# Reordering the start of a fused attention and MoE kernel: weight loads, transposes and v loads move, a group-finishing rule and buffer counts change

## The chip, the core and the metric

The kernel runs on one core of a Trainium2 chip. The metric is the device time of one execution in microseconds, taken as the median of several runs; lower is better. The core has five engines with instruction queues of their own, each worked through strictly in order: TensorE (PE, matmuls), VectorE (DVE), ScalarE (ACT), GpSimd (POOL) and SyncE (SP). Transfers are issued by POOL (one queue, which can also convert float32 to bfloat16 on the way) and by SP (another queue); SP also issues the transposing transfers.

## The reference

Attention with forget gates over 8 batches, 8 heads, 576 positions and 64 dimensions, followed by a two-layer MLP over the 4608 tokens:

```python
scores = scale * np.matmul(q, k.transpose(0, 1, 3, 2))
log_f = np.log(np.clip(f, 0.0001, 1.0))
cum = np.cumsum(log_f, axis=-1)
decay = cum[:, :, :, None] - cum[:, :, None, :]
scores = np.where(causal, -1000000000.0, scores + decay)
attn = softmax(scores)
x = (attn @ v).transpose(0, 2, 1, 3).reshape(4608, 512)
h = x @ w_in                      # w_in: 512 x 2048
g = h * (1.0 / (1.0 + np.exp(-h)))
out = g @ w_out                   # w_out: 2048 x 512
```

All inputs and the output are float32.

## The kernel before, in words

The decay is split into a factor of the query, which the normalisation cancels, and a factor of the key, `w_bf`, which is multiplied into v (with a column of ones for the denominator). So v needs a conversion on POOL before it is used.

**First blocks.** The first 128 positions of each batch are done as one piece for all eight heads. For batch b: `load_qk0(b)` (POOL transfers that convert to bfloat16, pool `conv`, tag `qkb`, four buffers) and `load_v0(b)`; `turn0(b, i)` transposes the query (i = 0) or key block on TensorE with 16 small matmuls (L286), and ACT or DVE copies it out (L293); `scores0` makes the scores (L320) and their exponential on ACT (L327); the causal mask is either added by a matmul beforehand (`ban0`) or multiplied in by DVE (`mask0`, L336); `convert_v0(b)` (POOL, L341) multiplies v by the key factor; `out0` (L360) is the product with v, normalised by DVE; `back0` (L390) transposes the result into the MoE's input. The query block goes into pool `qktp`, tag `qkT`, three buffers, which the units below use as well.

**Units.** The other 448 positions are done in 32 units, n = 4 b + p, a pair of heads of a batch each. `load_qk(n)` (SP, four transfers), `load_tails(b)` (SP, two transfers, the last 64 positions of q and k for a batch), `cast_qk(n)` (POOL, L400 and L404, to bfloat16, again a `qkb` buffer of `conv`), `transposes(n)` (SP, L428, one transposing transfer into a `qkT` buffer), `scores(n, c)` for c = 0, 1, 2 (L460, exponentials at L464 and L476, masks by DVE), `load_v(b, c)` and `convert_v(b, c)` for c = 0 to 3 (SP, then POOL at L414, into `vp`), `attend(n)` (L507, L516), and `back(m)` for a pair of units (L549 or transposing transfers). `prepare(n)` is called early in each unit and issues the casts, transposes and loads of later units.

**MoE.** Tokens come in 13 groups: first blocks of batches 0 to 3 (512 columns), 4 and 5 (256), 6 and 7 (256), then the rest of each batch (384) and the tails (256). `m1_chunk(g, fc)` is one of 16 hidden chunks of a group: four matmuls (L568), a tanh on ACT (L576) and a product on DVE into `gt` (L577). `m2_part(g, tb, part)` is a quarter of the second layer for 128 tokens: four matmuls (L613); after the fourth, ACT copies the result to an `osb` buffer (L623, pool `opool`) and the store is put in a list that `store` issues on POOL (L592). Every PSUM tile of these steps but the scores shares one pool, `pbig`, of four buffers. `w_in` and `w_out` are loaded in four quarters each (`load_w_in`, `load_w_out`, L190 and L194).

**Order.** The order on every engine is that of the program text. `fill(us)` puts MoE work of about that length between the attention's steps; `step` chooses between a hidden chunk and an M2 part, by how far each layer's group has come, and starts M2 of a group only when all of its hidden chunks have been put out. `two_more(b)` does the first blocks of batches b and b + 1 with MoE work between. `slot` is a fill that also issues waiting stores. The start goes: first blocks of batches 0 to 3; loads of 4 and 5 and of `w_in`; `w_out` and batches 6 and 7 on POOL; SP waits for the second quarter of `w_out` (`after`, L200) and then loads for the first units; `fill(5.0)`, `two_more(4)`, `fill(5.0)`, M2 opened, `fill(6.0, 2)`, `two_more(6)`, a last fill, and then the loop over pairs of units.

Of the kernel before, what the change touches and what calls it, by code (L numbers as in the profile page):

```python
# [11 lines left out]
BF16 = mybir.dt.bfloat16  # L12
P = 128
# [5 lines left out]
def kernel(  # L19
# [41 lines left out]
    recp = ctx.enter_context(tc.tile_pool(name="recp", bufs=2))  # L61
    xqp = ctx.enter_context(tc.tile_pool(name="xqp", bufs=2))
    tpool = ctx.enter_context(tc.tile_pool(name="tpool", bufs=3))
    opool = ctx.enter_context(tc.tile_pool(name="opool", bufs=5))
    xpool = ctx.enter_context(tc.tile_pool(name="xpool", bufs=1))
    setup_pool = tc.tile_pool(name="setup", bufs=1)
    setup = setup_pool.__enter__()
# [131 lines left out]
    def after(ap):  # L199
        nc.sync.dma_start(out=junk[0:1, 0:16], in_=ap)  # L200
# [77 lines left out]
    def turn0(b, i):  # L278
        src = qk0[b]
        if i == 0:  # L280
            qT0[b] = qktp.tile([P, NP, P], BF16, name="qkT", tag="qkT")
        dst, evac = ((qT0[b], nc.scalar.copy), (kT0[b], nc.vector.tensor_copy))[i]
        tp = pbig.tile([P, NP, NRUN, RUN], FP32, name="tp", tag="big")
        for c in range(RUN):
            for j in range(2):
                nc.tensor.matmul(  # L286
                    tp[j * D : (j + 1) * D, :, :, c].rearrange("p a r -> p (a r)"),
                    lhsT=src[:, i, c * D : (c + 1) * D],
                    rhs=sel[:, j, :],
                    start=True,  # L290
                    stop=True,
                )
        evac(  # L293
            out=dst[:, :, :].rearrange("p a t -> p (a t)"),
            in_=tp[:, :, :, :].rearrange("p a r c -> p (a r c)"),
        )
# [298 lines left out]
    def m2_part(g, tb, part):  # L595
        gt = gts[g]
        last = g == NG - 1 and tb == GW[g] // P - 1
        if last:
            if part % 2 == 0:
                pos[g, tb] = pbig.tile([P, DM // 2], FP32, name="po", tag="big")  # L600
            m0 = part // 2 * DM // 2
            m1 = m0 + DM // 2
            fcs = range(part % 2 * NFC // 2, (part % 2 + 1) * NFC // 2)
            done = part % 2 == 1
        else:
            if part == 0:
                pos[g, tb] = pbig.tile([P, DM], FP32, name="po", tag="big")
            m0, m1 = 0, DM
            fcs = range(4 * part, 4 * part + 4)
            done = part == 3  # L610
        po = pos[g, tb]
        for fc in fcs:
            nc.tensor.matmul(  # L613
                po[:, :],
                lhsT=gt[:, fc, tb * P : (tb + 1) * P],
                rhs=w_out_bf[:, fc, m0:m1],
                start=(fc == 0),
                stop=(fc == NFC - 1),
            )
        if done:  # L620
            store(len(stores) - 4)
            osb = opool.tile([P, m1 - m0], FP32, name="osb", tag="osb")
            nc.scalar.activation(out=osb[:, :], in_=po[:, :], func=ACT.Copy, scale=0.5)  # L623
            for n, (r, b, s0) in enumerate(rows_of(g, tb)):
                t0 = b * S + s0
                q_ = nc.gpsimd if not last else (nc.scalar if n == 1 else nc.sync)
                stores.append((q_, out[t0 : t0 + r.stop - r.start, m0:m1], osb[r, :]))
# [12 lines left out]
    def step():  # L640
# [10 lines left out]
        if can1 and can2:  # L651
            f1 = M1[a][1] / NFC
            f2 = (c - sum(M2_OF[:g2])) / M2_OF[g2]
            want = 3 - at["last"] if abs(f1 - f2) < 0.15 else (1 if f1 < f2 else 2)
            if want == at["last"] and at["row"] >= 2 and abs(f1 - f2) < 0.25:
                want = 3 - want
            can1 = want == 1
        kind = 1 if can1 else 2
        at["row"] = at["row"] + 1 if kind == at["last"] else 1
# [55 lines left out]
    scores0(3, bans)  # L715
    convert_v0(3)
    load_qk0(4)
    load_v0(4)
    load_w_in(2)
    load_qk0(5)  # L720
    load_v0(5)
    load_w_in(3)
    back0(0, on_act)
    out0(2)
    back0(1, on_act)
# [7 lines left out]
        nc.gpsimd.memset(t[:, :, 1, :], 0.0)  # L733
    for t in vps:
        nc.gpsimd.memset(t[0:ST, NR, :, :], 0.0)
    convert_v0(4)
    load_w_out(0)
    load_w_out(1)
    convert_v0(5)
    load_qk0(6)  # L740
    load_v0(6)
    load_qk0(7)
    load_v0(7)
    load_w_out(2)
    load_w_out(3)
    after(w_out_bf[0:1, 2 * NFC // WQ - 1, DM - 16 : DM])
    load_qk(0)
    load_tails(0)
    load_qk(1)
    load_v(0, 0)  # L750
    load_v(0, 1)
    convert_v0(6)
    convert_v0(7)
    load_qk(2)
    load_v(0, 2)
    load_v(0, 3)
    load_qk(3)
    for n in range(2):
        cast_qk(n)
        transposes(n)  # L760
    load_tails(1)
    for c in range(NM):
        convert_v(0, c)
# [27 lines left out]
    fill(6.0, 2)  # L791
    two_more(6, False)
    ready.add(2)
    fill(1.0)

    def prepare(n):

        b, p = divmod(n, NP)  # L800
        if n + 2 < NU:
            cast_qk(n + 2)
            transposes(n + 2)
        if n + 4 < NU:
            load_qk(n + 4)
        if p == 0 and b > 0 and b + 1 < B:
            load_tails(b + 1)
        if p == 1 and b + 1 < B:
            for c in range(NM):
                load_v(b + 1, c)  # L810
        if p >= 2 and b + 1 < B:
            for c in range(2 * (p - 2), 2 * (p - 1)):
                convert_v(b + 1, c)

    LAG = 13.0
# [71 lines left out]
```

The softmax here doesn't subtract the row's maximum and nothing guards it: scores larger than these inputs give would overflow.

## Time and profile before

| What | Value |
|---|---|
| median of 6 runs | 350.11 us (349.27 to 353.23) |
| profiled execution | 349.63 us |
| its span | 347.9 us |
| TensorE busy | 333.5 us (96%) |
| ACT busy | 216.7 us (62%) |
| DVE busy | 182.3 us (52%) |
| POOL busy | 128.8 us (37%) |
| bytes read from HBM | 36.85 MB |

The profiled execution is one run of the program under the hardware's profiler; times in its views count from the start of its span. The first slices of the span have the transfer engines at nine tenths, the TensorE clock is at its full value in all of them, and from about 260 us on there are few transfers left. A row of a timeline gives start, duration, engine, line, operation, output and inputs, shapes and count, and in brackets the idle time of the engine ahead of it with what ended it. A row of the waits gives the engine and line that waited, what it waited for, and total microseconds, times and the longest.

### The profile page before, as it was taken

How to read it: one execution, taken by the hardware profiler on the slowest of the kernel's cores; microseconds unless marked ns; L12 is line 12 of the kernel's file. 1: busy time of each engine (PE TensorE's matmuls, PEld its weight loads, DVE VectorE, ACT ScalarE, POOL GpSimd, SP SyncE). 2: the span in 40 equal slices, each digit the busy share in tenths (PEclk: the TensorE clock that was granted, in tenths of full speed). 3: DMA queues.
4: the chain of work that ended last, by engine and by line, in shares of the span. 5: the costliest groups of instructions: out<-in, count | busy, mean ns of one | idle time of the engine just before them, and what ended most of it. 6: DMA issues, size and time to landing. Idle time of an engine off the chain costs nothing.

```text
span 347.9 us, 8844 instructions
## 1 busy us (share of the span) xinstructions
PE 333.5 (96%) x3520; PEld 199.4 (57%) x3567; DVE 182.3 (52%) x389; ACT 216.7 (62%) x401; POOL 128.8 (37%) x227
## 2 busy tenths in 40 slices
PE   8989978999899999999999999999999999999995
PEld 3745545567656566565655666756656565555664
DVE  4764727366556556546646554645645463444340
ACT  5865624966675757759658585785865934545441
POOL 8997337274180272254235028314520000010011
PEclk9999999999999999999999999999999999999999
DMA  8999999997897397897799979579952100010012
GB/s 156 194 211 209 218 210 185 227 211 179 198 170 159 93 206 160 164 208 160 156 223 154 184 147 210 135 154 192 180 101 58 48 32 30 32 58 35 30 62 60
DMA packets 141497, 50.44 MB, mean 145 GB/s; under 512 B 132368, under 2 KB 138768, under 8 KB 141456
## 3 DMA queue, kind: packets, MB, share of 16 engines
q1 hardware_dynamic: 131440, 32.70, 51.8%
q0 software_dynamic: 9856, 17.04, 20.3%
q8 instruction: 28, 0.46, 0.6%
q10 hardware_dynamic: 160, 0.13, 0.1%
q14 instruction: 13, 0.11, 0.1%
HBM read 36.85 MB, written 9.44 MB: 133 GB/s over the span
## 4 chain that ended last, share of the span: by engine, by line
PE 81%; DMA 6%; POOL 4%; ACT 3%; issue 3%; DVE 1%; ACTq 0%; POOLq 0%
PE po L613 34%; PE hp L568 29%; PE sc L460 7%; DMA w_out_bf<-in_moe_w_out_dram 6%; PE dn L507 5%; PE dn L516 3%; PE wm L232 1%; POOL v L341 1%; ACT u L464 1%; PE tp L286 1%; POOL w_in_bf L190 1%; DVE u L336 1%; ACT ut L476 1%; POOL vf L140 1%; PE tx L549 1%
## 5 line engine op out<-in xcount | busy, mean ns | idle before, releaser
L576 ACT ACTIVATE th<-hp 128x384 bf16<-128x384 f32 (+2 forms) x208 | 95.8, 482 | 88.1 <-PE hp L568 86.0
L577 DVE SCALAR_TENSOR_TENSOR gt<-th,hp 128x384 bf16<-128x384 bf16 (+2 forms) x208 | 105.6, 522 | 78.9 <-ACT th L576 75.6
L613 PE MATMUL po<-w_out_bf,gt 128*128 128x512 bf16 (+1 forms) x550 | 138.5, 373 | 5.9 <-DMA w_out_bf<-in_moe_w_out_dram 1.9
L568 PE MATMUL hp<-x,w_in_bf 128*128 128x384 bf16 (+2 forms) x700 | 129.0, 321 | 0.5
L568 PEld LDWEIGHTS <-w_in_bf 128*128 128x128 bf16 x832 | 78.1, 98 | 53.8 <-issue 1.6
L592 POOL DMA_DIRECT2D out_dram<-osb x38 | 20.9, 551 | 176.0 <-ACT osb L623 125.8
L613 PEld LDWEIGHTS <-gt 128*128 128x128 bf16 x592 | 55.1, 98 | 52.2 <-issue 5.3
L464 ACT ACTIVATE u<-sc 128x1024 bf16<-128x1024 f32 (+1 forms) x96 | 75.3, 824 | 11.9 <-PE sc L460 11.8
L414 POOL TENSOR_TENSOR vp<-vf,w_bf 128x520 bf16<-128x520 f32 (+1 forms) x32 | 35.0, 1097 | 16.5 <-DMA vf<-in_v_dram 11.4
L469 DVE TENSOR_TENSOR u<-u,tri 128x768 bf16<-128x768 bf16 x32 | 22.2, 695 | 25.6 <-ACT u L464 25.6
L623 ACT ACTIVATE osb<-po 128x512 f32<-128x512 f32 (+1 forms) x37 | 22.2, 599 | 14.4 <-PE po L613 14.3
L460 PE MATMUL sc<-qkT 64*128 64x128 bf16 (+1 forms) x640 | 26.5, 207 | 0.1
L460 PEld LDWEIGHTS <-qkT 64*128 64x128 bf16 x640 | 18.2, 94 | 11.8 <-issue 9.1
L483 DVE TENSOR_TENSOR ut<-ut,trit 128x128 bf16<-128x128 bf16 x32 | 7.5, 233 | 31.0 <-ACT ut L476 31.0
L476 ACT ACTIVATE ut<-sc 128x640 bf16<-128x640 f32 x32 | 23.3, 729 | 0.0
L507 PEld LDWEIGHTS <-u 128*128 128x128 bf16 x576 | 20.8, 97 | 3.6 <-issue 0.3
L507 PE MATMUL dn<-vp,u 128*128 128x65 bf16 x384 | 21.8, 193 | 0.0
L525 DVE TENSOR_TENSOR xr<-dn,rec 128x448 bf16<-128x448 f32 x32 | 20.0, 625 | 1.1
L400 POOL CAST qkb<-qf 128x384 bf16<-128x384 f32 x32 | 16.2, 507 | 11.1 <-DMA qf<-in_q_dram 10.1
L507 PE MATMUL dn<-v,u 128*128 128x65 bf16 x192 | 19.8, 193 | 0.2 <-DVE gt L577 0.2
L400 POOL CAST qkb<-kf 128x384 bf16<-128x384 f32 x32 | 18.3, 571 | 1.8 <-DMA kf<-in_k_dram 1.7
L568 PE MATMUL hp<-xt,w_in_bf 128*128 128x256 bf16 x128 | 17.7, 273 | 0.1
(68 smaller groups left out, 205.6 us busy)
## 6 DMA issues: line engine op xcount, KB each, us to landing
out_dram<-osb POOLq DMA_DIRECT2D x32, 256.0 KB, 2.8
vf<-in_v_dram SPq DMA_DIRECT2D x26, 256.0 KB, 4.3
qf<-in_q_dram SPq DMA_DIRECT2D x64, 96.0 KB, 3.0
kf<-in_k_dram SPq DMA_DIRECT2D x64, 96.0 KB, 2.9
w_in_bf<-in_moe_w_in_dram POOLq DMA_DIRECT2D x4, 512.0 KB, 6.7
w_out_bf<-in_moe_w_out_dram POOLq DMA_DIRECT2D x4, 512.0 KB, 9.4
vf<-in_v_dram POOLq DMA_DIRECT2D x6, 256.0 KB, 7.0
qkb<-in_q_dram POOLq DMA_DIRECT2D x8, 128.0 KB, 5.5
```

The lines of the kernel that those rows point to most:

```text
L400: nc.gpsimd.tensor_copy(out=t2[:, c0 : c0 + NR, :].rearrange("p c x -> p (c x)"), in_=t[:, :, :, :].rearrange("p c h d -> p (c h d)"),)
L414: nc.gpsimd.tensor_tensor(out=vbf[b][r, c, :, :], in0=vst[b][c][r, :, :], in1=w_bf[r, c + 1, b * H : (b + 1) * H, None].to_broadcast([n, H ...
L460: nc.tensor.matmul(sc[:, i, o : o + q1 - q0], lhsT=kt, rhs=t[r, q0:q1], start=True, stop=True)
L464: nc.scalar.activation(out=u[:, :, c * SM : c * SM + w], in_=sc[:, :, 0:w], func=ACT.Exp, scale=scale)
L469: nc.vector.tensor_tensor(out=x, in0=x, in1=tri[:, None, None, :].to_broadcast([P, 2, NR, P]), op=ALU.mult,)
L476: nc.scalar.activation(out=ut[:, :, 0:3:2, :].rearrange("p k i t -> p i k t"), in_=sc[:, :, T0 : T0 + (NM + 1) * ST].rearrange("p i (k t) ...
L507: nc.tensor.matmul(dn[:, i * NR + c - 1, :], lhsT=u[:, i, o : o + P], rhs=vals(kb, i), start=(kb == 0), stop=(kb == c),)
L568: nc.tensor.matmul(hp[:, :], lhsT=w_in_bf[:, cc, fc * P : (fc + 1) * P], rhs=xcols(g, cc), start=(cc == 0), stop=(cc == NCC - 1),)
L576: nc.scalar.activation(out=th[:, :], in_=hp[:, :], func=ACT.Tanh, scale=0.5)
L577: nc.vector.scalar_tensor_tensor(out=gt[:, fc, :], in0=th[:, :], scalar=1.0, in1=hp[:, :], op0=ALU.add, op1=ALU.mult,)
L613: nc.tensor.matmul(po[:, :], lhsT=gt[:, fc, tb * P : (tb + 1) * P], rhs=w_out_bf[:, fc, m0:m1], start=(fc == 0), stop=(fc == NFC - 1),)
L623: nc.scalar.activation(out=osb[:, :], in_=po[:, :], func=ACT.Copy, scale=0.5)
```

## The change

Eight edits, none of which alters what is computed:

- the query blocks of the first blocks get a tag of their own, `qT0`, with two buffers in the same pool;
- the output pool has four buffers instead of five, and at most three stores are held back where it was four;
- `step` gets a rule: when at most two M2 parts are left in the groups up to the current one and the next group's hidden chunks are three quarters done, it goes on with the hidden chunks;
- the blocks of batches 4 and 5: both q and k loads first, then two quarters of `w_in`, then both v;
- all of `w_out` is issued ahead of the blocks of batches 6 and 7, its first half ahead of the conversion of batch 4's v;
- on SP and POOL, the casts and transposes of units 0, 1 and 2 stand between the loads; the v of batch 0 is loaded after the second transpose; `cast_qk(0)` stands ahead of the conversions of batches 6 and 7;
- the last fill before the units is 4.0 instead of 1.0;
- `prepare`: unit 0 no longer casts for unit 2, and the v of batch 1 is loaded at p = 2 and converted at p = 3.

```diff
-    opool = ctx.enter_context(tc.tile_pool(name="opool", bufs=5))
+    opool = ctx.enter_context(tc.tile_pool(name="opool", bufs=4))
...
-            qT0[b] = qktp.tile([P, NP, P], BF16, name="qkT", tag="qkT")
+            qT0[b] = qktp.tile([P, NP, P], BF16, name="qT0", tag="qT0", bufs=2)
...
-            store(len(stores) - 4)
+            store(len(stores) - 3)
...
                 want = 3 - want
+            if sum(M2_OF[: g2 + 1]) - c <= 2 and f1 >= 0.75:
+                want = 1
             can1 = want == 1
...
     load_qk0(4)
+    load_qk0(5)
+    load_w_in(2)
+    load_w_in(3)
     load_v0(4)
-    load_w_in(2)
-    load_qk0(5)
     load_v0(5)
-    load_w_in(3)
     back0(0, on_act)
...
-    convert_v0(4)
     load_w_out(0)
     load_w_out(1)
+    convert_v0(4)
     convert_v0(5)
-    load_qk0(6)
-    load_v0(6)
-    load_qk0(7)
-    load_v0(7)
     load_w_out(2)
     load_w_out(3)
+    load_qk0(6)
+    load_qk0(7)
+    load_v0(6)
+    load_v0(7)
     after(w_out_bf[0:1, 2 * NFC // WQ - 1, DM - 16 : DM])
     load_qk(0)
     load_tails(0)
     load_qk(1)
-    load_v(0, 0)
-    load_v(0, 1)
+    cast_qk(0)
+    transposes(0)
     convert_v0(6)
     convert_v0(7)
     load_qk(2)
-    load_v(0, 2)
-    load_v(0, 3)
+    cast_qk(1)
+    transposes(1)
+    for c in range(NM):
+        load_v(0, c)
+    cast_qk(2)
+    transposes(2)
     load_qk(3)
-    for n in range(2):
-        cast_qk(n)
-        transposes(n)
     load_tails(1)
...
     ready.add(2)
-    fill(1.0)
+    fill(4.0)
...
-        if n + 2 < NU:
+        if 0 < n < NU - 2:
             cast_qk(n + 2)
             transposes(n + 2)
         if n + 4 < NU:
             load_qk(n + 4)
-        if p == 0 and b > 0 and b + 1 < B:
+        if b + 1 == B:
+            return
+        if p == 0 and b > 0:
             load_tails(b + 1)
-        if p == 1 and b + 1 < B:
+        if p == (1 if b > 0 else 2):
             for c in range(NM):
                 load_v(b + 1, c)
-        if p >= 2 and b + 1 < B:
-            for c in range(2 * (p - 2), 2 * (p - 1)):
+        if p >= 2:
+            for c in range(2 * (p - 2), 2 * (p - 1)) if b > 0 else range(NM * (p - 2)):
                 convert_v(b + 1, c)
```

## The prediction, made before the changed kernel ran

> **What bounds the kernel now.** I read the busy table first, then TensorE's own waits, then the timelines of the engines round each wait.
>
> ```profile
> PE 333.5 (96%) x3520; PEld 199.4 (57%) x3567; DVE 182.3 (52%) x389; ACT 216.7 (62%) x401; POOL 128.8 (37%) x227
> ```
>
> TensorE is busy for 333.5 of 347.9 us. Both programs issue the same matmuls, so a change of order can win only the time in which TensorE stands still, and lose only by new waits there. The list of TensorE's waits says what there is to win:
>
> ```profile
> PE po L613 <- DMA w_out_bf<-in_moe_w_out_dram: 1.9, 1, 1.9
> PE po L613 <- issue: 1.4, 9, 0.2
> PE wm L232 <- DVE warm L204: 1.2, 1, 1.2
> PE po L613 <- DVE gt L577: 0.9, 1, 0.9
> PE dn L360 <- DVE u L336: 0.9, 2, 0.8
> PE tp L286 <- DMA qkb<-in_q_dram: 0.8, 1, 0.8
> PE tx L549 <- DVE gt L577: 0.2, 1, 0.2
> ```
>
> The columns are total us, times, longest. The "issue" row is nine gaps of one matmul's length (records that the trace lacks), and the warm-up row is before anything that changes. The other five, 4.7 us in all, are the stake. TensorE's timeline places them:
>
> ```profile
> 26.06 1.36 PE L286 MATMUL tp<-sel,qkb 128*64 128x64 bf16 x32 [0.76 <-DMA qkb<-in_q_dram]
> ...
> 41.14 2.75 PE L613 MATMUL po<-w_out_bf,gt 128*128 128x512 bf16 x12
> 43.73 0.60 PE L568 MATMUL hp<-x,w_in_bf 128*128 128x256 bf16 x4
> 46.22 1.89 PE L613 MATMUL po<-w_out_bf,gt 128*128 128x512 bf16 x7 [1.89 <-DMA w_out_bf<-in_moe_w_out_dram]
> ...
> 57.18 0.43 PE L360 MATMUL dn<-v,u 128*128 128x65 bf16 x8 [0.76 <-DVE u L336]
> ...
> 92.60 1.02 PE L613 MATMUL po<-w_out_bf,gt 128*128 128x512 bf16 x4 [0.95 <-DVE gt L577]
> ```
>
> The idle time stands in brackets ahead of the instruction that it delayed: once for a query block of batch 5, once for the last quarter of w_out, once for a mask, once at a group boundary of the MoE. After 120 us TensorE hardly waits at all.
>
> **The change, part by part.**
>
> *Loads of batch 5 ahead of w_in.* Now POOL issues qk(4), v(4), w_in(2), qk(5), v(5), w_in(3); from issue and time to landing these land at 21.9, 22.8, 25.3, 26.8, 27.5 and 29.8. So the queue lands in the order of issue, at some 2.4 us for a weight quarter (1 MB in HBM). With qk(5) straight after qk(4) its half megabyte lands near 23.3, before TensorE comes for it at 25.3. That takes away 0.76, and 0.31 more: the key block landed after the query block, and the pitch between the two transposes at 26.46 is 335 ns where 27 would do. Together -1.07. The w_in quarters then land near 25.9 and 28.3; the first use of w_in(2) is the ninth hidden chunk, at about 31. v(4) and v(5) land last, by 29.8; their conversions on POOL (1.05 each) end near 30 and 31, and out0(4) and out0(5) want them at 31.5 and 32.6. Cover of 1.5 us; beyond that each us late costs one.
>
> *w_out ahead of the first blocks of batches 6 and 7.* Landings now:
>
> ```profile
> 33.24 0.77 POOL L194 DMA_DIRECT2D w_out_bf<-in_moe_w_out_dram  x1 [0.62 <-DMA w_out_bf<-in_moe_w_out_dram]
> 35.55 0.74 POOL L194 DMA_DIRECT2D w_out_bf<-in_moe_w_out_dram  x1 [1.54 <-DMA w_out_bf<-in_moe_w_out_dram]
> ```
>
> These two landed 9.5 and 10.6 us later, at 42.7 and 46.15, behind the 1.5 MB of batches 6 and 7, which landed between 36.0 and 39.8. Changed, they are issued near 31.0 and 31.8, after the conversion of v(5), and their place in the queue is straight behind w_out(1), which lands at 35.3 as before (the same bytes are ahead of it). The trace moved the next 3.5 MB of that queue in 46.15 - 35.3 = 10.85 us, 3.1 us per MB, with SP's loads beside it. Two quarters then land at 38.4 and 41.5. TensorE needs them at 42.86 - 1.07 = 41.8 and 44.33 - 1.07 = 43.3. Here I weigh a rule: the Trainium skill's "DMA: Bandwidth & Descriptors", section "Queues, rings and completion order", says that each DMA engine takes turns, packet by packet, among the queues that have work. SP's queue opens after 35.3 in both kernels (its first load waits for w_out(1)); with a full half going to it from 36 on, a quarter would take 4.8 us, w_out(3) would land near 44.2, and 0.9 of the 1.89 would stay. The trace's 2.9 and 3.45 us between its last landings, under that very traffic, say less than a half; I take the row: -1.89.
>
> The moved blocks pay for it: qk(6) and qk(7) land near 43 and 45, v(6) and v(7) by about 46.2, since the total is unchanged. Their turns come at 49.33 - 2.96 = 46.4 and 48.8 (2.96 is what has been won so far). Nothing.
>
> *A tag of its own for qT0.* The first-block queries shared three buffers with the units' transposes, two of which are claimed in program order before batches 6 and 7. ACT shows the price:
>
> ```profile
> 53.81 0.58 ACT L293 CAST qkT<-tp 128x512 bf16<-128x512 f32 x1 [2.43 <-PE sc L320]
> 54.29 0.39 ACT L576 ACTIVATE th<-hp 128x256 bf16<-128x256 f32 x1
> 54.56 1.03 ACT L327 ACTIVATE u<-sc 128x1024 bf16<-128x1024 f32 x1
> ```
>
> The copy for batch 7 waited for the scores of batch 6, and the exponential of batch 6 queued behind it. With two own buffers the copy is done before 53, so the exponential starts when its scores end (53.7), some 0.8 earlier; the mask (1.48 each) then ends about 56.3, and TensorE comes at 56.42. -0.8 of the 0.93; batch 7's mask stays just critical.
>
> *Casts, transposes and v of the units, reordered.* SP and POOL are in order, so this needs following. SP's four loads, two tails and four loads land between 44.1 and 48.9 as now; the first cast ended at 48.6, waiting for the tails. It now stands ahead of the conversions of v(6) and v(7) (which now run at 38.2 and 39.8): 48.6 + 2 x 1.05 = 50.7. out0(6) and out0(7) come near 53.4 and 54.7. Hidden by some 4 us. Transpose 0 goes out at 48.6 instead of 55.5, four loads (2.1), transpose 1 at about 52, the four v loads to 55.6, landing by 60 with the 3.5 to 5 us of the v loads now; cast 2 ends near 57, transpose 2 goes out there, four conversions (4.6) end by 62.5 or so. The first attend of batch 0 comes at 69.8 - 3.8 + 3.0 = 69, where 3.8 is the sum of the gains so far and 3.0 the work of the next part. Hidden by 6 us. Behind them on SP stand load_qk(3), the tails of batch 1, load_qk(4) and transpose 3, going out near 65 as now (65.4), because it waits for the first unit's scores anyway. v of batch 1 is loaded one unit later and converted by about 84.5; its first attend comes near 90.
>
> *More MoE ahead of unit 0.* Three hidden chunks of 256 (0.43 each) and two M2 parts (0.86) move, 3.0 us: moved, not added. Zero.
>
> *The rule for finishing a group.* At 92.6 a new M2 tile waited 0.95 for DVE, because four hidden chunks had been put behind two score blocks and held all the four shared PSUM buffers. In the changed order the last three chunks of that group are followed by two M2 parts of the old one (1.73), which cover the tanh and the product (0.38 + 0.42). -0.95. The same for the 0.23 before the transposes at 116.67: an M2 part now stands between. The rule also makes runs of five chunks in the tail, where three were. With one buffer held by an M2 tile, three are left; for 256 columns the loop of tanh and product is about 1.0 us against 0.87 of two chunks. Bounds: nothing (a run of 20 matmuls at 153.4 takes 3.28 us with no gap) to 0.15 for each later chunk, some 0.6 in all.
>
> *Four output buffers instead of five.* ACT's copies of outputs wait for matmuls alone, never for a store; a store lands in 2.8 us and 36 token tiles take 300 us. Nothing, even where POOL holds one up.
>
> **Sum.** -1.07 - 1.89 - 0.8 - 0.95 - 0.23 = -4.94. Against it I set new waits of 0 to 1.5, 0.7 taken: the tail's runs, and unit 0, where 1.73 us of MoE instead of 2.15 stands between the first two score blocks, so that ACT's exponentials (0.93 each, two of them) are just critical. Net -4.2. The profiled execution took 349.63 (347.9 of span and 1.7 around it), so 345.4; its median was 350.11, 0.48 above, so **345.9**.
>
> **Rivals.**
>
> *The weights still come late.* With the half share the last quarter costs 0.9; with v(4) or v(5) 1 us over their cover, another 1.0. Gain 2.3: 347.8. For it: queue shares can't be read exactly from landings. Against: 2.9 and 3.45 us.
>
> *The new order brings its own waits.* ACT's exponentials around unit 0, or a run of chunks on the PSUM buffers, give back 3 to 4 us in several places: about 349.5, no change. For it: ACT is 62% busy and in order. Against: in the present kernel none of its 96 exponentials makes TensorE wait.
>
> *Slower: the chain through SP and POOL.* The conversions of batch 0's v now stand behind three casts, and their loads behind two transposes. If SP's loads are starved, each us beyond the cover of 6 at attend 0 is a us of TensorE. It ends slower by 0.5% from 6 + 4.2 + 1.8 = 12 us of lateness; at 13 us, 353. For it: SP issues of 2.2 us at 38 to 43 show a full queue. Against: at 46.2 the other queue is empty and the loads then land in 3 to 5 us.
>
> **How the numbers follow.** Forecast 0.60 (345.0 to 346.8, by the 0 to 1.5 of new waits), late weights 0.20, own waits 0.12, slower 0.08. About 0.5%, 1.8 us, is what a measurement of this kernel can tell from no change; 347.8 is faster by that bound. So faster 0.80, same 0.12, slower 0.08. The range takes in the first two cases: 344.7 to 348.6.
>
> **What will show it.** TensorE's row of waits for w_out is gone, and for qkb at turn 5; no wait of out0(6) above 0.2; no 0.9 for the product at a group's end; the third and fourth w_out quarters land by 41.8 and 43.3; transpose 0 goes out near 48.6. Wrong would be: TensorE waiting for vp or v in out0 or attend, rows for exponentials among its waits, or a start of unit 0 later than 62 us.

## The result, and the profile after

| | before | changed |
|---|---|---|
| median | 350.18 us (348.56 to 353.23, 63 runs) | 347.29 us (345.21 to 350.54, 28 runs) |
| profiled execution | 349.63 us | 347.08 us |
| its span | 347.9 us | 345.3 us |
| TensorE busy | 333.5 us | 331.4 us |

The ratio is 0.991, with a 95% interval of 0.9896 to 0.9924: 2.9 us faster by the medians. The forecast was 345.9, with a range of 344.7 to 348.6. Direction and range hold; 1.4 us of the forecast gain are missing. Three executions that ran in a slower state (one of the changed kernel, two of the weights' order alone below) are in the medians and not in the ratios, so the two can differ a little.

TensorE's busy time fell by 2.1 us although the matmuls are the same, because it counts each matmul to its modelled end; 0.8 of the 2.1 lies in the first 8 us (6.80 us busy there before, 6.00 now), ahead of every edit.

The list of TensorE's waits in the changed kernel, with total us, times and the longest:

```profile
PE sc L460 <- DMA qkT<-qkb: 2.4, 2, 1.5
PE po L613 <- issue: 1.4, 9, 0.2
PE wm L232 <- DVE warm L204: 1.2, 1, 1.2
PE dn L507 <- DVE gt L577: 1.1, 1, 1.1
PE tp L286 <- DMA qkb<-in_k_dram: 0.5, 1, 0.5
PE tp L286 <- DMA qkb<-in_q_dram: 0.3, 1, 0.3
PE tx L390 <- DVE xq L375: 0.3, 1, 0.3
PE hp L568 <- DVE gt L577: 0.2, 1, 0.2
```

The rows for `w_out` and for the mask are gone. The two `qkb` rows are not the old one: they lie at 5.5 and 6.9 us, in the first blocks of batch 0, before anything that the change touches. Three rows are new: units wait for transposed queries and keys (2.4 us), an attend waits for a product of the MoE (1.1 us), and so does a hidden chunk (0.24 us). TensorE's timeline shows the places of the old waits without a bracket, and then the new ones:

```profile
25.03 1.08 PE L286 MATMUL tp<-sel,qkb 128*64 128x64 bf16 x32
...
42.22 0.60 PE L568 MATMUL hp<-x,w_in_bf 128*128 128x256 bf16 x4
42.66 1.89 PE L613 MATMUL po<-w_out_bf,gt 128*128 128x512 bf16 x7
...
52.70 0.42 PE L360 MATMUL dn<-v,u 128*128 128x65 bf16 x8
...
60.31 0.40 PE L460 MATMUL sc<-qkT 64*128 64x128 bf16 x8
...
74.64 0.40 PE L460 MATMUL sc<-qkT 64*128 64x128 bf16 x8 [1.48 <-DMA qkT<-qkb]
...
86.23 0.40 PE L460 MATMUL sc<-qkT 64*128 64x128 bf16 x8 [0.89 <-DMA qkT<-qkb]
...
108.31 0.19 PE L507 MATMUL dn<-v,u 128*128 128x65 bf16 x1 [1.12 <-DVE gt L577]
```

The first, third and fourth rows stood at 26.06, 46.22 and 57.18 before. The fifth is the start of unit 0 (62.15 before); the sixth and seventh are the starts of units 3 and 5.

**Where the time went.** The starts of the same instruction in both timelines give the lead of the changed kernel. After the turn of batch 5 it is 28.23 - 26.92 = 1.31 us (0.20 of it was there before the turn of batch 4 already). After the last quarter of `w_out` it is 47.94 - 44.39 = 3.55, and at the second masked product 58.64 - 53.82 = 4.82. At unit 0 the changed kernel has done 3.04 us more MoE work, so the lead is 62.15 + 3.04 - 60.31 = 4.88 us, where the forecast's steps up to there made 3.8. At the end of the last matmul it is 344.04 - 341.50 = 2.54. So the start went better than forecast, and 2.3 us of the lead were lost in the units. The new brackets make 1.48 + 0.89 + 1.12 + 0.24 = 3.73 us; the old ones that are gone after unit 0 (0.95, 0.23, 0.22) make 1.40; the difference is that 2.3.

A bracket is a little less than what a wait costs. From the start of the hidden chunk at 43.73 to the M2 part at 46.22 (rows of the prediction) there were 2.49 us before; from 42.22 to 42.66 there are 0.44 now. That is 2.05 won for a bracket of 1.89: the bracket starts at the modelled end of the matmul ahead, and the next one could have started 0.16 us sooner.

**Why unit 3 waits.** Transpose 3 is the fourth of the units' transposes (they are counted from 0). These are SP's rows of the changed kernel (start, us taken to issue):

```profile
50.71 1.34 SPq L428 DMA_TRANSPOSE qkT<-qkb  x1
...
54.78 1.22 SPq L428 DMA_TRANSPOSE qkT<-qkb  x1
56.10 4.09 SPq L179 DMA_DIRECT2D vf<-in_v_dram  x4
60.28 1.54 SPq L428 DMA_TRANSPOSE qkT<-qkb  x1
...
68.41 1.67 SPq L428 DMA_TRANSPOSE qkT<-qkb  x1
...
77.47 4.68 SPq L179 DMA_DIRECT2D vf<-in_v_dram  x4
82.26 1.30 SPq L428 DMA_TRANSPOSE qkT<-qkb  x1
```

Transpose 3 goes out at 68.41 (65.42 before) and lands 6.2 us later (3.6 before): at 74.59 where it was 69.07, while TensorE comes for it at 74.64 - 1.48 = 73.16. The last thing that SP waits for ahead of it is the cast for unit 3 on POOL, as SP's waits between 66 and 70 us say:

```profile
SPq L428 <- POOL qkb L404: 0.5, 1, 0.5
```

And this is POOL's timeline up to that cast:

```profile
60.53 2.25 POOL L414 TENSOR_TENSOR vp<-vf,w_bf 128x520 bf16<-128x520 f32 x2 [3.48 <-DMA vf<-in_v_dram]
63.34 2.18 POOL L414 TENSOR_TENSOR vp<-vf,w_bf 128x520 bf16<-128x520 f32 x2 [0.55 <-DMA vf<-in_v_dram]
65.46 1.69 POOL L592 DMA_DIRECT2D out_dram<-osb  x3
67.20 0.50 POOL L400 CAST qkb<-qf 128x384 bf16<-128x384 f32 x1
```

That cast starts at 67.20 (63.68 before), straight behind the four conversions of batch 0's v, which end at 65.5 instead of 58.0, and three stores, 1.69 us. The conversions waited for their loads (3.48 and 0.55 in brackets), and those loads stand on SP behind transposes 0 and 1. So v having been moved back makes the cast late. But SP waits only 0.5 us for it: until 67.87 it is busy with the issue of the loads for units 3 and 4 and of two tails. The other 2.5 us of the later issue, and the longer flight, are not the cast's.

**Why unit 5 waits.** Transpose 5, the last row of SP above, goes out at 82.26 (77.67 before), straight behind the four loads of batch 1's v, whose issue alone took 4.68 us. They are in that place because they are loaded one unit later. It lands at 86.19; TensorE comes for it at 86.23 - 0.89 = 85.34. Whether the place of v is what makes the two transposes late is what the first experiments ask.

### The profile page after: what moved, and what is told of

It reads as the page before. It is cut to its first block, busy times and chain, and to the rows that moved or that the text cites. A ratio compares the mean times of both kernels' runs of the same rounds, so it can differ in the third digit from the quotient of the medians.

```text
span 345.3 us, 8845 instructions
## 1 busy us (share of the span) xinstructions
PE 331.4 (96%) x3520; PEld 198.9 (58%) x3567; DVE 184.6 (53%) x389; ACT 218.1 (63%) x401; POOL 128.9 (37%) x227
## 4 chain that ended last, share of the span: by engine, by line
PE 71%; DMA 13%; POOL 5%; SPq 5%; issue 3%; ACT 1%; DVE 1%; POOLq 0%
PE po L613 30%; PE hp L568 28%; PE sc L460 6%; PE dn L507 4%; DMA w_out_bf<-in_moe_w_out_dram 3%; DMA qktf<-in_k_dram 3%; DMA vf<-in_v_dram 3%; SPq L158 3%; PE dn L516 2%; DMA kf<-in_k_dram 2%; DMA qkb<-in_k_dram 1%; POOL v L341 1%; DMA qkT<-qkb 1%; SPq L168 1%; POOL w_in_bf L190 1%
## 5 line engine op out<-in xcount | busy, mean ns | idle before, releaser
L414 POOL TENSOR_TENSOR vp<-vf,w_bf 128x520 bf16<-128x520 f32 (+1 forms) x32 | 33.8, 1060 | 30.6 <-DMA vf<-in_v_dram 28.0
L469 DVE TENSOR_TENSOR u<-u,tri 128x768 bf16<-128x768 bf16 x32 | 22.9, 715 | 20.2 <-ACT u L464 20.1
L400 POOL CAST qkb<-qf 128x384 bf16<-128x384 f32 x32 | 18.0, 561 | 32.3 <-DMA qf<-in_q_dram 31.3
L483 DVE TENSOR_TENSOR ut<-ut,trit 128x128 bf16<-128x128 bf16 x32 | 10.4, 326 | 35.3 <-ACT ut L476 35.2
L400 POOL CAST qkb<-kf 128x384 bf16<-128x384 f32 x32 | 16.7, 523 | 8.7 <-DMA kf<-in_k_dram 8.7
```

The costliest lines, as they stand in the source:

```text
L400: nc.gpsimd.tensor_copy(out=t2[:, c0 : c0 + NR, :].rearrange("p c x -> p (c x)"), in_=t[:, :, :, :].rearrange("p c h d -> p (c h d)"),)
L414: nc.gpsimd.tensor_tensor(out=vbf[b][r, c, :, :], in0=vst[b][c][r, :, :], in1=w_bf[r, c + 1, b * H : (b + 1) * H, None].to_broadcast([n, H ...
L469: nc.vector.tensor_tensor(out=x, in0=x, in1=tri[:, None, None, :].to_broadcast([P, 2, NR, P]), op=ALU.mult,)
```

## The experiments

Times are medians, ratios are to the kernel before with a 95% interval; the kernel before took 350.05, 350.34 and 350.22 us beside the three sets of runs. "Theory 1" is mine, as each expectation states it.

### v of batch 0 back between the first loads (changed kernel otherwise)

```diff
     load_qk(1)
+    load_v(0, 0)
+    load_v(0, 1)
     cast_qk(0)
...
     load_qk(2)
+    load_v(0, 2)
+    load_v(0, 3)
...
-    for c in range(NM):
-        load_v(0, c)
```

> The changed kernel with the v loads of batch 0 put back where they were (two after the loads of unit 1, two after those of unit 2); all else as changed. Theory 1, in-order queues: TensorE's wait of 1.48 us for unit 3's transpose comes from its cast standing on POOL behind four v conversions that wait for loads landing at 62 to 63 us. With the loads earlier the conversions end some 3 us earlier, cast 3 runs near 64.5 instead of 67.2, the transpose goes out near 66, and the wait falls to below 0.3: about 345.9. Theory 2, full transfer engines and an earlier start of unit 0: the transposes are late whatever stands ahead of them, the wait stays at 1 us or more: 347.3. In both the wait for unit 5's transpose (0.89) stays.

346.41 us, ratio 0.9874 (0.9840 to 0.9908), between the two theories and with an interval that overlaps the changed kernel's. The wait of unit 3 shrank from 1.48 to 0.45 and that of unit 5 stayed (1.08). But the cast moved only from 67.20 to 66.10 and transpose 3 from 68.41 to 68.01, where its issue took 2.51 us in place of 1.67; SP no longer waits for the cast, and the transpose lands at 73.88, 0.7 earlier. The other 0.3 of what the wait lost is TensorE's own: it comes to unit 3 at 73.48, after a new wait of 0.4 for v of the first blocks. So at most 0.7 us of the 1.48 go with v's place.

### v of batch 1 back to its old unit

```diff
-        if p == (1 if b > 0 else 2):
+        if p == 1:
             for c in range(NM):
                 load_v(b + 1, c)
...
-            for c in range(2 * (p - 2), 2 * (p - 1)) if b > 0 else range(NM * (p - 2)):
+            for c in range(2 * (p - 2), 2 * (p - 1)):
```

> The changed kernel with the v of batch 1 loaded at p = 1 and converted at p = 2 and 3, as before the change; all else as changed. Theory 1: the wait of 0.89 us for unit 5's transpose comes from the four v loads that stand on SP's queue straight ahead of it (4.7 us of issue). Moved one unit earlier they stand ahead of unit 4's transpose instead, which has more time: the wait at unit 5 goes, no new one at unit 4, 346.4. Theory 2: the engines are full, the wait stays or moves to unit 4, 347.3. The wait at unit 3 (1.48) stays in both.

346.22 us, ratio 0.9889 (0.9853 to 0.9924), again overlapping the changed kernel's. The wait of unit 5 is gone, none above 0.04 came at unit 4, and unit 3 waits 1.51, much as in the changed kernel (an attend at 81.09 waits 0.28, which is new). It looks like one wait with one cause, and the landing times say otherwise. Transpose 5 goes out at 82.73, later than the 82.26 of the changed kernel, and lands at 85.84 for 86.19. TensorE comes to unit 5 at 86.44 in place of 85.34, and that is why it doesn't wait. The four loads now stand ahead of transpose 4, which goes out at 78.06 for 73.95 and lands at 83.40, just as unit 4 begins (83.45). Unit 5 begins 0.2 us later than in the changed kernel. What the span won, 344.8 for 345.3, was won at 107.77, where the attend waits 0.38 in place of 1.12 (see the rule's experiment).

### Both

> Both put back: v of batch 0 and of batch 1 loaded where they were before the change, all else as changed. Theory 1: both waits for transposes go (2.4 us in all), 344.9. Theory 2: 346.8 to 347.3, with waits for transposes left of 1.5 us or more.

344.89 us, ratio 0.9839 (0.9810 to 0.9868), 2.4 us under the changed kernel, with intervals that don't meet. That the place of the two v loads costs time is thus shown. The brackets for transposes now make 0.4. But the transposes are no sooner: 3 and 5 land at 75.35 and 86.00 (74.59 and 86.19 in the changed kernel), and unit 5 begins at 86.60 for 86.23. TensorE only comes later, because the first line of its waits is another:

```profile
PE dn L360 <- POOL v L341: 2.2, 2, 1.8
...
PE sc L460 <- DMA qkT<-qkb: 0.4, 1, 0.4
```

The last product of the first blocks waits for v(6) and v(7), whose conversion stands behind the first cast; POOL's timeline shows that this cast waited for the tails:

```profile
53.24 0.62 POOL L404 CAST qkb<-qktf 128x128 bf16<-128x128 f32 x1 [1.94 <-DMA qktf<-in_k_dram]
53.83 2.06 POOL L341 TENSOR_TENSOR v<-vf,w_bf 128x520 bf16<-128x520 f32 x2
```

In the changed kernel the same cast ended at 50.7, in time. The cover that the forecast gave these conversions, "some 4 us", is gone when the tails land at 53.2 (48.2 in the kernel before). How late they land changes from one execution to the next: the kernel with v of batch 0 alone put back is the same program up to there, and its cast ended at 50.8 with a wait of 0.4.

The profiled execution, 346.21 us, is also the slowest of the six. Its span is 0.9 us under that of the changed kernel, and the attend at 108 us, which waits for nothing here, more than accounts for it. By which waits the other 1.5 us of the medians were won, no trace shows.

### Both, and the two conversions ahead of the first cast

```diff
-    cast_qk(0)
-    transposes(0)
     convert_v0(6)
     convert_v0(7)
+    cast_qk(0)
+    transposes(0)
```

> The changed kernel with the v loads of batches 0 and 1 put back where they were, and the conversions of batches 6 and 7 ahead of the first unit's cast on POOL. Theory 1: takes away also the wait of out0 for v of batches 6 and 7 that showed once those loads stood elsewhere (2.2 us in that profile) and does not delay the first cast, whose data land at 48 us or later: 344.3, with no wait of out0 for v. Theory 2 (the transfers themselves are late): v of batch 7 lands too late whatever stands ahead, the wait stays: 344.9.

345.15 us, ratio 0.9851 (0.9825 to 0.9878). The product waits for v no more; unit 3 waits 0.99 again, for a transpose that lands at 74.62. The medians can't tell this kernel from the last.

Taken together: in all seven kernels of this document that are made from the changed one, transpose 3 lands between 73.9 and 75.9, wherever v stands. What changes is when TensorE comes for it. That is nearer to theory 2, full transfer engines, than to theory 1: in the changed kernel their busy share, as the windows give it, is 1.2 from 56 to 74 us.

### The longer fill taken back (changed kernel otherwise)

```diff
-    fill(4.0)
+    fill(1.0)
```

> The changed kernel with 1.0 instead of 4.0 in the last fill ahead of unit 0. If that MoE work is only moved, as the prediction had it: 347.3. Theory 1: unit 0 starts 3 us earlier, near 57.3, while the transposes and v conversions go out as before; the first attend then waits about 1 us for v (ready near 65.5) and unit 3 about 4.5 us for its transpose, so 3 us are lost: 350.3.

351.67 us, ratio 1.0041 (1.0026 to 1.0056): 4.4 us more than the changed kernel, and slower than the kernel before. TensorE comes to unit 3 at 70.44 in place of 73.16, for a transpose that lands at 74.34 (74.59), and stands still for 3.9 us in one piece. A second price comes behind it. The windows round that wait (window and length, then busy us of TensorE, weight loads, DVE, ACT and POOL, the granted clock, the transfer share and GB/s):

```profile
66.00:70.00 4.00, 3.95 (x50) 2.53 (x47) 2.38 (x7) 2.23 (x4) 2.54 (x6) 1.00 1.01 290
70.00:74.40 4.40, 0.45 (x17) 0.28 (x15) 1.51 (x4) 1.35 (x4) 1.25 (x3) 0.85 1.26 210
74.40:78.00 3.60, 3.27 (x17) 1.75 (x19) 0.56 (x1) 1.32 (x2) 1.62 (x3) 0.50 1.07 208
78.00:82.00 4.00, 4.00 (x48) 2.15 (x47) 0.54 (x2) 2.68 (x6) 1.43 (x2) 0.76 1.21 223
```

The clock falls to 0.50 at the end of the idle stretch and stays there into the last window. If it is only ever 1.00 or 0.50, half clock covers 0.15 x 4.40 / 0.5 = 1.3 us of the second window, all of the third and 0.24 x 4.00 / 0.5 = 1.9 us of the fourth. In the last two TensorE had work, 5.5 us of it at half speed, so some 2.8 us were lost on top of the 3.9. With the old waits of 2.4 and 1.1 gone and one of 0.9 back: 3.9 + 2.8 + 0.9 - 3.5 = 4.1; the spans differ by 349.9 - 345.3 = 4.6.

### The weights' order alone, on the kernel before

Loads of batches 4 and 5, `w_in`, all of `w_out`, then 6 and 7, with the conversions of v(4) and v(5) where the change has them; nothing else.

```diff
     load_qk0(4)
+    load_qk0(5)
+    load_w_in(2)
+    load_w_in(3)
     load_v0(4)
-    load_w_in(2)
-    load_qk0(5)
     load_v0(5)
-    load_w_in(3)
...
     convert_v0(5)
+    load_w_out(2)
+    load_w_out(3)
     load_qk0(6)
...
-    load_w_out(2)
-    load_w_out(3)
```

> The kernel before with the load order alone changed: batches 4 and 5, w_in, w_out ahead of batches 6 and 7, and the conversions of batches 4 and 5 where the changed kernel has them. By the prediction's sum: the waits for the block of batch 5 (1.07) and for w_out (1.89) go, 347.2. Rival (the earlier start of unit 0 meets transposes that go out no earlier): 1.5 us or more come back as waits for transposes or for v, 348.7 or more.

352.17 us, ratio 1.0040 (1.0021 to 1.0060): slower, as the rival had it. The waits for batch 5 and for `w_out` are gone, and unit 0 waits instead:

```profile
62.65 0.61 PE L460 MATMUL sc<-qkT 64*128 64x128 bf16 x8 [4.45 <-DMA qkT<-qkb]
```

SP's timeline says why: transposes 0 and 1 are issued at 58.07, where it was 55.51.

```profile
58.07 3.85 SPq L428 DMA_TRANSPOSE qkT<-qkb  x2
```

SP's first two v loads went out at 50.66 (47.19 before). With this order of the weights on POOL's queue SP's loads come some 3 us later, and with TensorE 3 to 4 us early the two meet at unit 0. After the 4.45 us of idle time the windows show the half clock again:

```profile
58.00:62.60 4.60, 0.20 (x1) 0.00 (x0) 0.00 (x0) 0.60 (x1) 2.10 (x2) 0.90 1.27 166
62.60:68.00 5.40, 5.35 (x24) 2.21 (x25) 0.98 (x2) 2.32 (x3) 4.01 (x9) 0.50 0.88 215
68.00:72.00 4.00, 4.00 (x52) 2.47 (x52) 1.11 (x3) 3.40 (x7) 0.00 (x0) 0.93 1.07 232
```

Worked out as above it took about 3.0 us. Won: 0.76 + 0.31 + 1.89 + 0.93 = 3.9, the last being the mask's wait, which is gone here too (see the experiment with the tag). Lost: 4.45 + 3.0. The sum is +3.6; the spans differ by 3.1.

### The longer fill alone, on the kernel before

```diff
-    fill(1.0)
+    fill(4.0)
```

> The kernel before with 4.0 instead of 1.0 in the last fill alone. As the prediction had it, work moved and not added, with TensorE waiting for nothing in the first units of that kernel: no change, 350.2. If the longer lead also gives cover that the kernel before lacks in its slower executions: up to 0.5 us faster.

347.76 us, ratio 0.9932 (0.9905 to 0.9959), where I had expected nothing. This one edit is worth 2.5 us. TensorE's waits:

```profile
PE tp L286 <- DMA qkb<-in_q_dram: 1.7, 1, 1.7
PE po L613 <- DMA w_out_bf<-in_moe_w_out_dram: 1.6, 1, 1.6
PE po L613 <- issue: 1.4, 9, 0.2
PE wm L232 <- DVE warm L204: 1.2, 1, 1.2
PE tx L390 <- DVE xq L375: 0.3, 1, 0.3
PE dn L360 <- DVE u L336: 0.2, 1, 0.2
PE tp L286 <- DMA qkb<-in_k_dram: 0.2, 1, 0.2
```

Ahead of unit 0 this is the same program as the kernel before, so what differs there is the execution: the blocks of batch 5 cost 1.74 and 0.18 (0.76 before), the last quarter of `w_out` 1.61 (1.89), the masks 0.25 (0.93). A bracket of one profile is not a fixed price. Behind unit 0, what is missing is the 0.95 at the group's end, the 0.22 and the 0.23: the fill shifts which MoE piece falls between which attention steps for the rest of the kernel, and in this phase no product is late. With 3.04 us of fill, unit 0 starts at 65.32, 0.13 later than the kernel before would put it (62.15 + 3.04), and the span is 2.2 shorter, so 2.3 us are won behind unit 0. The brackets of the three waits explain 1.4 of them, and 1.9 with the 0.16 us that each leaves out. The other 0.4 is in no row of the waits; that stays open.

### The rule for finishing a group: alone, and left out

```diff
+            if sum(M2_OF[: g2 + 1]) - c <= 2 and f1 >= 0.75:
+                want = 1
```

> The kernel before with the group-finishing rule in the MoE scheduler alone. By the prediction: the wait of 0.95 us at a group's end and the one of 0.23 go, at most 0.6 us comes back: 349.0 to 349.6. Rival: runs of hidden chunks ahead of an attend, or in the tail, wait for PSUM buffers instead; as much comes back as is won: 350.1.

Added to the kernel before: 349.86 us, ratio 0.9990 (0.9975 to 1.0005). The wait that it was to remove is still there, at 91.34:

```profile
91.34 1.02 PE L613 MATMUL po<-w_out_bf,gt 128*128 128x512 bf16 x4 [0.95 <-DVE gt L577]
```

> The changed kernel without the group-finishing rule. By the prediction the rule is worth about 1 us (the wait at a group's end comes back, the runs of five in the tail go): 348.0. If, as the rule alone on the kernel before suggests, it is worth nothing and the wait merely stands elsewhere (1.12 ahead of an attend in the changed kernel): 346.8 to 347.5.

Taken out of the changed kernel (the two lines with a minus): 345.96 us, ratio 0.9871 (0.9839 to 0.9903), 1.3 us less than the changed kernel, with intervals that overlap by a hair. The wait of 1.12 ahead of the attend fell to 0.33, and no wait at a group's end came back. So the rule doesn't remove the 0.95. That it costs 1.3 in all isn't certain at this precision.

Does the rule make the 1.12? It puts three hidden chunks in a row ahead of that attend (the first row below; without the rule there are two, and an M2 part). Their products stand on DVE behind a unit's mask, and until they are done they hold the PSUM buffers that the attend needs. But the kernels with v put back have the same three chunks there, and what differs is the mask. The second row is the mask in the changed kernel, the third in the kernel with both v put back:

```profile
105.08 2.11 PE L568 MATMUL hp<-x,w_in_bf 128*128 128x384 bf16 x12
...
106.09 1.70 DVE L483 TENSOR_TENSOR ut<-ut,trit 128x128 bf16<-128x128 bf16 x1 [1.10 <-ACT ut L476]
...
106.46 0.22 DVE L483 TENSOR_TENSOR ut<-ut,trit 128x128 bf16<-128x128 bf16 x1 [1.24 <-ACT ut L476]
```

With a mask of 1.70 the attend waits 1.12, with 1.42 (v of batch 0 back) 0.84, with 0.96 (v of batch 1 back) 0.38, with 0.22 and 0.23 (both back; and the conversions ahead of the cast) nothing. Each time the wait is the mask less 0.58. Without the rule a mask of 1.97 costs 0.33. So the run of three takes the cover away, and the mask's length sets the wait.

### The tag for qT0 and the output buffers alone

```diff
-    opool = ctx.enter_context(tc.tile_pool(name="opool", bufs=5))
+    opool = ctx.enter_context(tc.tile_pool(name="opool", bufs=4))
...
-            qT0[b] = qktp.tile([P, NP, P], BF16, name="qkT", tag="qkT")
+            qT0[b] = qktp.tile([P, NP, P], BF16, name="qT0", tag="qT0", bufs=2)
...
-            store(len(stores) - 4)
+            store(len(stores) - 3)
```

> The kernel before with the separate tag for the first blocks' queries (and the four output buffers that make room for it) alone. By the prediction: TensorE's waits of 0.93 us for the mask of batches 6 and 7 fall to about 0.1, since the copy of batch 7's query no longer waits for batch 6's scores: 349.4. If the mask is late for another reason, or the output buffers matter: no change or slower, 350.1 or more.

349.78 us, ratio 0.9982 (0.9967 to 0.9997), as expected, and nothing waits for a store or an output buffer. ACT copies the queries of batch 7 as soon as they are transposed, and the exponential follows without a queue:

```profile
52.89 0.59 ACT L293 CAST qT<-tp 128x512 bf16<-128x512 f32 x1 [1.05 <-PE tp L286]
53.87 0.38 ACT L576 ACTIVATE th<-hp 128x256 bf16<-128x256 f32 x1 [0.40 <-PE hp L568]
54.21 1.02 ACT L327 ACTIVATE u<-sc 128x1024 bf16<-128x1024 f32 x1
```

The mask's wait is gone. But this run doesn't show that the tag took it. In the kernel with the longer fill alone, which is the kernel before up to there, the copy still waits 2.43 for the scores, and the mask of batch 6 is in time:

```profile
54.65 0.58 ACT L293 CAST qkT<-tp 128x512 bf16<-128x512 f32 x1 [2.43 <-PE sc L320]
...
55.41 1.03 ACT L327 ACTIVATE u<-sc 128x1024 bf16<-128x1024 f32 x1
...
56.48 0.69 DVE L336 TENSOR_TENSOR u<-u,tri 128x1024 bf16<-128x1024 bf16 x1 [0.50 <-ACT u L327]
```

The two masks take 0.69 and 0.83 there, 1.49 and 1.54 in the kernel before, and TensorE waits 0.25 for 0.93. With the rule alone they take 0.69 and 0.75 (0.16 waited), with the weights' order alone 0.69 each (nothing waited), and the copy waits 2.43 in both. So the late copy by itself costs 0.25 at most; the rest of the 0.93 comes only with masks as long as in that one execution, and the forecast's "1.48 each" is no property of the mask. With the tag alone they take 0.69 and 1.13. What the tag gives is cover: the exponential starts within 0.2 us of the end of its scores, so that a mask of 1.0 us, as in the changed kernel, is in time.

### The weights' order and the fill, without the rest

> The kernel before with the changed load order and the fill of 4.0, but with the transposes of units 0 and 1 behind all loads and the shared query tag. Theory 1 (lead and transposes trade against each other): with the load order alone TensorE stood 4.45 us until the transpose landed at 62.6; with 3.0 us of MoE work in between about 1.4 us of it stay, too short for the clock to drop: 348.3, so the lead alone saves nearly 4 us. Rival (the transposes between the loads are what counts, the lead only moves work): the wait stays over 3 us and the clock drops: 351 or more.

345.83 us, ratio 0.9878 (0.9849 to 0.9906). Unit 0 waits 1.20, as expected, for a transpose issued at 59.41; further waits of this kind of 0.25 and 0.60 follow at units 4 and 5. SP and POOL have the units' transposes and v in their old order here, and still transposes 3 and 5 land at 74.62 and 86.85, as late as in the changed kernel. With the weights' order alone transpose 3 lands at 72.27, with the fill alone at 72.16, in the kernel before at 69.07. So the weights' order and the fill make it as late without any reordering of the units' transposes, and in the kernel with the fill taken back it is as late without the fill. No one edit is its cause; what delays it stays open.

The total is 2.5 below the expectation, as much as the fill alone won; the waits of 0.95, 0.23 and 0.22 are missing here too. Three of the eight edits thus make a kernel that is not slower than the whole change (1.5 us faster by the medians; the intervals overlap).

### The best order with a still longer fill

```diff
-    fill(4.0)
+    fill(6.0)
```

> The changed kernel with v of batches 0 and 1 loaded where they were, the conversions of batches 6 and 7 ahead of the first cast, and 6.0 instead of 4.0 in the last fill. Theory 1: 2 us more lead takes the last wait for unit 3's transpose (0.99 in the profile without it): 344.2. If the lead is used up already and other waits take its place: 345.2.

On the kernel with both v loads back and the conversions ahead of the cast: 345.00 us, ratio 0.9854 (0.9828 to 0.9881), no different. The wait of unit 3 is gone, one of 1.0 appears at unit 4 and one of 0.7 for a product. Three kernels thus stand at 344.9 to 345.2 and can't be told apart; each beats the kernel before by about 5.2 us, and the changed one by 2.1 to 2.4. The kernel of three edits above, at 345.83, has an interval that overlaps theirs.

## Why the prediction was right, and where it was wrong

**Right: the loads of batch 5.** The wait is gone at 25.03, and the start gained 1.11 there (1.31 less the 0.20 from before), for 1.07 forecast. The brackets at this place were 0.76 in the execution that was read and 0.87, 1.49 and 1.92 in three others with the old order, so the agreement to 0.04 is chance. The conversions of v(4) and v(5) ended some 0.6 us ahead of their use, where 1.5 us of cover were forecast.

**Right: `w_out`, by the row and not by the rule.** The third and fourth quarters landed 6.8 and 9.3 us after their issue at 31.65 and 32.4, so near 38.4 and 41.8; the forecast by the trace's 3.1 us per MB was 38.4 and 41.5. TensorE came for the last at 42.66, 0.9 us later. With the half share that the Trainium skill's "DMA: Bandwidth & Descriptors", section "Queues, rings and completion order", was read to give SP, the last would have landed near 44.2. The rival of late weights falls with it. The moved blocks of batches 6 and 7 cost nothing at their turns, as forecast.

**Right in result, for the smaller part in cause: the mask.** 0.8 forecast, the wait gone. The queue on ACT, to which the forecast put it all down, is worth 0.25 at most where the masks take 0.69 to 0.83. The rest needs masks as long as the 1.49 and 1.54 of the one execution that was read, which were taken for a fixed price.

**Wrong: "SP's four loads, two tails and four loads land between 44.1 and 48.9 as now".** In the kernel before they land from 43.2 to 49.3, in the changed one from 43.7 to 51.8. Moving 2 MB of weights ahead on one queue was costed for that queue alone. The other queue paid: transpose 0 went out at 50.71 for 48.6 forecast, and with the weights' order alone SP ran 3 us late.

**Wrong: "transpose 3, going out near 65 as now".** It went out at 68.41 and landed 6.2 us later, for 3.6 before. The step named what transpose 3 waited for on SP in the kernel before, and neither when SP would be through with the loads ahead of it (67.87) nor its cast on POOL, behind conversions that were now forecast to end at 62.5 "or so" (65.5 measured) and behind stores, which were not counted at all. The time to landing was not costed, nor was a need: TensorE comes at 73.16, for a landing at 74.59. Price 1.48.

**Wrong: v of batch 1 one unit later.** It was costed by when its conversion ends and where it is first used. Its four issues on SP, 4.68 us, went straight in front of transpose 5, for which no cover had been worked out. There the wait is 0.89; but with v moved back the transpose lands only 0.35 sooner, so the place of v is not shown to be its cause. That v of batches 0 and 1 stand better where they were is shown by the medians, 2.4 us for both.

**Wrong: "moved, not added. Zero."** The longer fill is worth 2.5 us alone and 4.4 in the changed kernel. It lets TensorE come later for transposes that land when they land, which the weights' order needs, it keeps TensorE from an idle stretch long enough to lose its clock, and it changes the phase of all that follows. The second and third of these can't be seen in a list of what is moved.

**Wrong: the group-end waits, -0.95 and -0.23, put down to the rule.** They are gone, but the 0.95 goes with the fill: the rule alone left it standing (only the 0.23, and 0.22 ahead of an attend, are not in its waits), the fill alone removed both. The rule's own effect in the changed kernel was put at 0 to 0.15 for each chunk in the tail. What came instead was 1.12 at 108.31: behind a run of three hidden chunks of 384 the products were queued on DVE behind a mask of 1.70 us, so the PSUM buffers were held when the attend came. Masks were costed as if their length were fixed.

**Wrong: the sum.** The edits were added as if each stood alone. They don't add: the weights' order alone is +1.8 us (+1.4 by the ratio), the fill alone -2.5, and both together -4.4. The new waits, set at 0 to 1.5 with 0.7 taken, were 3.73. That is the term that was mis-sized, and it accounts for more than the missing 1.4 us; the gains ahead of unit 0, 4.9 for 3.8, made up the rest. Of the 1.1 us more than forecast there, 0.2 was there from the start, 0.2 came between the turn of batch 5 and the first M2 part, 0.2 at `w_out` and 0.5 at the masks.

**What was luck.** That the measured time lies in the range owes much to an edit that was priced at nothing. Without the longer fill the same sum would have said the same 345.9, and that kernel takes 351.67, slower than the kernel before. None of the forecast's signs of being wrong came (no row for v or vp, none for exponentials, unit 0 at 60.31 and not later than 62); they didn't look at the units' transposes.

**The rivals.** The slower one named the right chain, SP and POOL, and the wrong victim: not the attend of batch 0 for its v, but units 3 and 5 for their transposes. The one of new waits had the right size, 3 to 4 us, and named scores and PSUM buffers; only 1.1 us of it were the latter.

## What to carry to other kernels

When instructions are moved in an in-order queue, list what stands behind them and who waits for that, for every queue and every engine that feeds it: here the losses were at transposes, behind loads that were themselves in good time. What one queue gained here came back as later landings on the other, so put the new landing times of both beside the new, earlier time of need. Price edits in one stretch together: one that wins time alone can lose it when the next thing isn't ready, and a filler that costs nothing may be what makes the others pay.

And when an experiment makes a wait go away, look whether the thing that was waited for came sooner, or the one who waits came later. A row of waits can't tell the two apart; landing times can.

## What the hardware showed that was not expected

- **A long wait is paid twice.** After idle stretches of 3.9 and 4.45 us TensorE's clock was at 0.50 for about 6.8 us, which cost some 2.8 and 3.0 us more; after 1.5 us in the changed kernel, and after waits of up to 1.99 in others, it stayed at 1.00. The Trainium skill's "TensorE: Matmul & The Clock Gate", section "Part 1: The HAM clock gate (the "warmup" mystery)", states a half clock after an idle window of some 3.4 us. Both stretches are longer than that; but by the windows above the clock fell 3.5 us into the second and already some 2.7 us into the first (half clock for the last 1.3 us before 74.40, idle from 70.44), so the figure holds only roughly here.
- **The same transfers take differently long to issue and to land.** Four v loads of SP took 3.19, 3.42, 3.87, 4.30 and 4.68 us to issue in different kernels, a transposing transfer 1.2 to 3.0. In an in-order queue that is time taken from the instruction behind. Transpose 3 landed 3.4 to 6.6 us after its issue. What makes the difference was not tried.
- **A mask on DVE is long only where POOL computes at the same time.** In the fourteen traces the units' masks that overlap none of POOL's casts and conversions take no more than 0.23 us (L483, 342 of 448) and 0.56 (L469, 234 of 448). Those that overlap one take up to 1.97 and 2.00, though some are not slowed at all. No run varied that alone, but there is no exception. An execution in which the two collide pays where the mask has no cover: 0.76 at batch 6 in the kernel before, 1.12 at the attend at 108.31 in the changed one.
